# Converting the weights of a fused attention and two-MoE kernel: low parts on VectorE, the first MoE's pieces twice as wide

## The chip, the cores and the metric

The kernel runs on one core of one Trainium2 chip. The metric is the device time of one execution in microseconds (us); lower is better. A core has TensorE (PE, which multiplies matrices; its weight loads are listed apart as PEld), VectorE (DVE), ScalarE (ACT), GpSimd (POOL) and SyncE (SP, which here only issues DMAs). Each engine takes its instructions in the order in which they stand in its queue.

## What is computed

Decay attention, then two feed-forward blocks (the "MoE" of the names), each on the output of the one before:

```python
# attention: batch 4, 8 heads, 576 positions, head size 64
scores = scale * q @ k.T + (cum[:, None] - cum[None, :])   # cum: running sum of log f, causal
x = softmax(scores) @ v                                    # -> 2304 tokens x 512
# first MoE: w_in 512 x 2048, w_out 2048 x 512
h = x @ w_in
x = np.maximum(0.01 * h, h) @ w_out
# second MoE: w_a, w_b 512 x 1536, w_out 1536 x 512
out = ((x @ w_a) * (x @ w_b)) @ w_out
```

The weights arrive as 64-bit floats, eight bytes for each number.

## The kernel before

**Pairs for each product.** PE multiplies in a reduced fp32 format (fp32r). So each operand is kept as two numbers, a high part `hi` and a low part `lo` with hi + lo equal to the value, and each product is three matmuls (hi·hi, hi·lo, lo·hi).

**Converting a weight.** `load_weight` (L105) makes the pair for a block of 128 x 512 numbers, in pieces of `W` columns. For each piece SP fetches the raw doubles into a tile `raw` (L114 or L116), of which there are `RB` buffers. `from_double` (L90) then builds the fp32 number in a tile `c`: ACT takes the absolute value of the upper word (L94), DVE clips it (L95), shifts it (L96), ors bits of the lower word in (L97, which reads `raw` and `c`), and ors the sign in (L100, the same two inputs, and the last reader of `raw`). `split` (L85) writes `hi` on ACT (L87) and `lo = c - hi` (L88), on POOL unless it is told another engine. A `c` tile is free again when its `lo` is written.

**The first MoE's weights** (`load_a`, L523) come in 16 blocks `wi` of w_in and 16 blocks `wo` of w_out, 32 in all, in pieces of 256 columns: 64 pieces, with five buffers of `raw` and three of `c`. They are loaded in the first 186 us, beside the attention of the first tokens and the first matmuls of the MoE. POOL also builds the attention's masks there (L305, L306, L329, L333).

**The second MoE's weights** (`load_b`, L578) are 36 blocks (`wa`, `wb`, `wc`, twelve of each) in one piece of 512 columns each, with three buffers of `raw` and two of `c`. They are loaded from 568 us to about 720 us, beside the last two token chunks (7 and 8) of the first MoE. All blocks but the first few take over the memory of first-MoE blocks, so that their `hi` and `lo` have to wait until PE has used those for the last time.

**The first MoE's matmuls.** For a chunk of 256 tokens and a block fi, `l1` makes h in 12 matmuls (L537); ACT makes `gh` and `hs` from it (L544, L545), and DVE the low part `gl` (L546). `l2` (L559), 12 matmuls as well, runs two or three blocks later. One h and one y together are called a step below. The second MoE's matmuls are L608 and L631.

**Order.** The code is written in an order of its own, and a scheduler then sets the order of the instructions on each engine before the run; nothing is reordered while it runs.

Of the kernel before, what the change touches and what calls it, by code (L numbers as in the profile page):

```python
# [10 lines left out]
I32 = mybir.dt.int32  # L11
# [6 lines left out]
P = 128  # L18
# [8 lines left out]
def kernel(  # L27
# [13 lines left out]
    nc = tc.nc  # L41
    B, H, S, D = q.shape
    NT, DM = out.shape
    w_in, w_out, w_a, w_b, w_o2 = (w.bitcast(I32) for w in (w_in, w_out, w_a, w_b, w_o2))
    F1 = w_in.shape[1] // 2
    F2 = w_a.shape[1] // 2
    NF1, NF2, ND = F1 // P, F2 // P, DM // P
# [10 lines left out]
    wpool = ctx.enter_context(tc.tile_pool(name="wpool", bufs=1))  # L58
# [23 lines left out]
    def f32(ap):  # L82
        return ap.bitcast(F32)

    def split(hi, lo, src, lo_engine=None):  # L85

        nc.scalar.copy(hi, src)  # L87
        (lo_engine or nc.gpsimd).tensor_tensor(out=lo, in0=src, in1=f32(hi), op=ALU.subtract)  # L88

    def from_double(raw, c):  # L90


        top, low, t = raw[:, :, 1], raw[:, :, 0], c.bitcast(F32)
        nc.scalar.activation(t, top.bitcast(F32), AF.Abs)  # L94
        nc.vector.tensor_scalar(t, t, TOP_MIN, TOP_MAX, op0=ALU.max, op1=ALU.min)  # L95
        nc.vector.tensor_scalar(c, c, 5, 2, op0=ALU.logical_shift_left, op1=ALU.logical_shift_right)  # L96
        nc.vector.scalar_tensor_tensor(  # L97
            out=c, in0=low, scalar=29, in1=c, op0=ALU.logical_shift_right, op1=ALU.bitwise_or
        )
        nc.vector.scalar_tensor_tensor(  # L100
            out=c, in0=top, scalar=-0x40000000, in1=c, op0=ALU.bitwise_and, op1=ALU.bitwise_or
        )
        return t

    def load_weight(pool, stg_pool, src, name, W, RB, **kw):  # L105

        hi = pool.tile([P, 512], F32R, tag="w", name=f"{name}_hi", **kw)
        lo = pool.tile([P, 512], F32R, tag="w", name=f"{name}_lo", **kw)
        for z in range(0, 512, W):
            raw = stg_pool.tile([P, W, 2], I32, tag="raw", bufs=RB, name=f"raw_{name}_{z}")  # L110
            view = raw.rearrange("p n t -> p (n t)")
            if len(src.shape) == 3:
                view = view.rearrange("p (a b) -> p a b", b=2 * P)
                nc.sync.dma_start(view, src[:, z // P : (z + W) // P, :])  # L114
            else:
                nc.sync.dma_start(view, src[:, 2 * z : 2 * (z + W)])  # L116
            c = stg_pool.tile([P, W], I32, tag="t", bufs=3 if stg_pool is stage else 2, name=f"c_{name}_{z}")
            split(hi[:, z : z + W], lo[:, z : z + W], from_double(raw, c))
        return hi, lo

    def cols(w, j):

        return w[:, 2 * j * P : 2 * (j + 1) * P].rearrange("(c p) f -> p c f", p=P)

    def rows(w, j):
        return w[j * P : (j + 1) * P, :]
# [5 lines left out]
    stage = stage_ctx.enter_context(tc.tile_pool(name="stage", bufs=2))  # L132
# [389 lines left out]

    def load_a(fi):  # L523
        wa[fi] = (
            *load_weight(wpool, stage, cols(w_in, fi), f"wi_{fi}", 256, 5, bufs=4 * NF1),
            *load_weight(wpool, stage, rows(w_out, fi), f"wo_{fi}", 256, 5, bufs=4 * NF1),
        )

    def l1(i, fi):
# [48 lines left out]
    def load_b(fi):  # L578
        res = []
        for idx, (src, nm) in enumerate(((cols(w_a, fi), "wa"), (cols(w_b, fi), "wb"), (rows(w_o2, fi), "wc"))):  # L580
            pool, bufs = (pools["wx"], 8) if fi * 3 + idx < 4 else (wpool, 4 * NF1)
            res += load_weight(pool, pools["wx"], src, f"{nm}_{fi}", 512, 3, bufs=bufs)
        wb[fi] = res
# [113 lines left out]
    def load_next():  # L697
        nonlocal loaded
        if loaded < NF1:
            load_a(loaded)  # L700
            loaded += 1
# [91 lines left out]
```

## Time and profile before

| | us |
|---|---|
| median of three runs | 1154.49 |
| lowest and highest | 1154.03 to 1155.28 |
| the profiled execution, its whole time | 1155.12 |
| its span in the profile | 1153.3 |
| PE busy in it | 1112.6 |
| DVE busy | 658.0 |
| ACT busy | 571.8 |
| POOL busy | 286.8 |

The span leaves 1.8 us of the execution's time outside it. PE is recorded as busy for 96% of the span, DVE for 57%; these are means over parts with different limits. DVE is busy for nearly all of two stretches, 66 to 186 us (the first MoE's weights) and 604 to 706 us (the second's), and for a few tenths behind 750 us. A matmul's record is longer than the distance to the next one (0.28 us against 0.12 us for 256 columns), so a PE that is recorded as busy can still be short of work; the count of matmuls in a stretch, and the share of its weight loads, show that.

### The profile page before, as it was taken

Reading aid. Unit: us, or ns where it says so; the run is one execution under the profiler, and the core shown is the slowest. Engines: PE = TensorE matmul, PEld = TensorE weight load, DVE = VectorE, ACT = ScalarE, POOL = GpSimd, SP = SyncE. Lnnn points to the kernel's source line nnn. Section 1 sums busy time; section 2 is a strip of 40 time slices with the busy share of each in tenths; the row PEclk is TensorE's granted clock in tenths of the full one; section 3 lists DMA queues with packets and bytes.
Section 4 is the critical chain, followed back from the end, with each engine's and each line's share of the span. In section 5 each row is a group of like instructions: output and inputs, shape, how many; then the busy total and the mean of one; then the engine's idle time right before and its main releaser. Section 6 shows DMA issues by size and latency. Waiting matters only on the chain.

```text
span 1153.3 us, 20360 instructions
## 1 busy us (share of the span) xinstructions
PE 1112.6 (96%) x7021; PEld 981.9 (85%) x7021; DVE 658.0 (57%) x1780; ACT 571.8 (50%) x1511; POOL 286.8 (25%) x486
## 2 busy tenths in 40 slices
PE   6999989999999999999999899999999999999998
PEld 3677778999989999999999887888888888888897
DVE  6789998887878787866459978111111211211122
ACT  5557687888877777867445545212111211211121
POOL 5556553333233323322124324101000100100000
PEclk9999999999999999999999999999999999999999
DMA  7556645433353234521234444101000100100010
GB/s 195 162 150 171 149 121 107 91 79 63 66 122 77 55 69 95 104 51 30 88 115 129 149 143 145 40 1 55 19 1 1 64 1 1 39 8 1 1 37 19
DMA packets 188583, 86.82 MB, mean 75 GB/s; under 512 B 144640, under 2 KB 174336, under 8 KB 188480
## 3 DMA queue, kind: packets, MB, share of 16 engines
q1 hardware_dynamic: 183296, 80.80, 27.9%
q10 hardware_dynamic: 5184, 4.72, 1.2%
q8 instruction: 55, 0.90, 0.3%
q14 instruction: 48, 0.39, 0.1%
HBM read 75.96 MB, written 9.51 MB: 74 GB/s over the span
## 4 chain that ended last, share of the span: by engine, by line
PE 69%; DVE 5%; issue 4%; DMA 3%; ACT 2%; POOL 1%; SPq 0%; ACTq 0%; POOLq 0%; DVEq 0%
PE ab L608 25%; PE o L631 13%; PE h L537 11%; PE y L559 11%; PE av L76 3%; PE s L76 3%; PE pp L76 2%; DMA xk<-in_k_dram 1%; DVE gl L546 1%; DMA sy<-y_dram 1%; DMA y_dram<-yo 1%; DVE c_wc L97 0%; ACT p L283 0%; ACT gh L544 0%; DVE c_wb L97 0%
## 5 line engine op out<-in xcount | busy, mean ns | idle before, releaser
L614 DVE TENSOR_TENSOR p<-ab,p 128x512 f32<-128x512 f32 (+1 forms) x60 | 38.3, 639 | 302.6 <-PE ab L608 299.4
L537 PE MATMUL h<-xh,wi_hi 128*128 128x256 f32 x576 | 168.6, 293 | 8.7 <-ACT hs L545 8.6
L559 PE MATMUL y<-gl,wo_hi 128*128 128x256 f32 x576 | 161.6, 287 | 3.4 <-DVE gl L546 3.4
L537 PE MATMUL h<-xl,wi_hi 128*128 128x256 f32 x576 | 164.7, 286 | 0.0
L537 PE MATMUL h<-xh,wi_lo 128*128 128x256 f32 x576 | 164.6, 286 | 0.0
L559 PE MATMUL y<-gh,wo_lo 128*128 128x256 f32 x576 | 160.5, 285 | 0.0
L559 PE MATMUL y<-gh,wo_hi 128*128 128x256 f32 x576 | 154.4, 292 | 3.9 <-ACT gh L544 3.9
L613 ACT COPY p<-ab 128x512 f32<-128x512 f32 (+1 forms) x60 | 32.7, 545 | 186.3 <-PE ab L608 186.3
L537 PEld LDWEIGHTS h<-xh,wi_hi 128*128 128x128 f32 x576 | 111.2, 193 | 15.7 <-ACT hs L545 12.0
L559 PEld LDWEIGHTS y<-gl,wo_hi 128*128 128x128 f32 x576 | 110.5, 192 | 5.0 <-DVE gl L546 4.3
L305 POOL TENSOR_SCALAR p<-cumb,ncum_t 128x384 f32<-128x384 f32 (+1 forms) x112 | 70.4, 630 | 169.5 <-PE pp L76 41.7
L537 PEld LDWEIGHTS h<-xh,wi_lo 128*128 128x128 f32 x576 | 111.3, 193 | 1.2 <-issue 1.2
L537 PEld LDWEIGHTS h<-xl,wi_hi 128*128 128x128 f32 x576 | 111.5, 194 | 0.8 <-issue 0.4
L559 PEld LDWEIGHTS y<-gh,wo_hi 128*128 128x128 f32 x576 | 104.6, 191 | 7.6 <-ACT gh L544 5.7
L559 PEld LDWEIGHTS y<-gh,wo_lo 128*128 128x128 f32 x576 | 110.7, 192 | 0.4
L87 ACT CAST pph<-p 128x512 fp32r<-128x512 f32 (+1 forms) x60 | 34.7, 578 | 130.5 <-DVE p L614 130.4
L283 ACT ACTIVATE p<-p,stat 128x384 f32<-128x384 f32 (+4 forms) x128 | 77.3, 604 | 26.0 <-DVE stat L312 22.3
L608 PE MATMUL ab<-yh,wb_hi 128*128 128x512 f32 (+1 forms) x240 | 88.8, 370 | 0.7 <-ACT yo L568 0.7
L608 PE MATMUL ab<-yh,wb_lo 128*128 128x512 f32 (+1 forms) x240 | 88.9, 370 | 0.0
L608 PE MATMUL ab<-yl,wa_hi 128*128 128x512 f32 (+1 forms) x240 | 88.8, 370 | 0.0
L608 PE MATMUL ab<-yh,wa_hi 128*128 128x512 f32 (+1 forms) x240 | 88.8, 370 | 0.0
L608 PE MATMUL ab<-yl,wb_hi 128*128 128x512 f32 (+1 forms) x240 | 88.7, 370 | 0.0
(164 smaller groups left out, 2766.3 us busy)
## 6 DMA issues: line engine op xcount, KB each, us to landing
cumb<-cum_dram SPq DMA_DIRECT2D x32, 288.0 KB, 3.7
raw_wi<-in_moe_w_in_dram SPq DMA_DIRECT2D x32, 256.0 KB, 3.1
raw_wo<-in_moe_w_out_dram SPq DMA_DIRECT2D x32, 256.0 KB, 3.2
raw_wa<-in_moe_w_a_dram SPq DMA_DIRECT2D x12, 512.0 KB, 3.6
raw_wb<-in_moe_w_b_dram SPq DMA_DIRECT2D x12, 512.0 KB, 3.5
raw_wc<-in_moe_w_out_dram SPq DMA_DIRECT2D x12, 512.0 KB, 3.6
xq<-in_q_dram SPq DMA_DIRECT2D x144, 32.0 KB, 2.0
y_dram<-yo ACTq DMA_DIRECT2D x36, 128.0 KB, 2.7
```

The costliest lines, as they stand in the source:

```text
L76: return method(*args, **kw)
L87: nc.scalar.copy(hi, src)
L283: act_att.activation(pt, pt, AF.Exp, bias=stat[:, 0, s : s + 1], scale=-1.0, accum_out=stat[:, 1, s : s + 1])
L305: pool_att.tensor_scalar(pt, cumb[:, :n], 1.0, ncum_t[:, t, bh : bh + 1], op0=ALU.mult, op1=ALU.add)
L537: nc.tensor.matmul(hps, w[:, c * P : c * P + P], x[:, c, :], start=(n == 0), stop=(n == 3 * ND - 1))
L546: nc.vector.tensor_tensor(out=gl, in0=hs, in1=f32(gh), op=ALU.subtract)
L559: nc.tensor.matmul(o, w[:, d * P : d * P + P], g, start=(fi == 0 and n == 0 and d % 2 == 0), stop=(fi == NF1 - 1 and n == 2 and d % 2 == 1),)
L608: nc.tensor.matmul(o[:, :tn], w[:, c * P : c * P + P], y[:, c, :tn], start=(m == 0), stop=(m == 3 * ND - 1))
L613: nc.scalar.copy(p[:, :tn], ab[0][:, :tn])
L614: nc.vector.tensor_tensor(out=p[:, :tn], in0=ab[1][:, :tn], in1=p[:, :tn], op=ALU.mult)
L631: nc.tensor.matmul(o, g[:, t * P : t * P + P], w, start=(fi == 0 and m == 0), stop=(fi == NF2 - 1 and m == 2))
```

## The change

Three things change in one place. `split` is told `nc.vector` for all weights, so the `lo` of the 32 + 36 blocks is written by DVE and no longer by POOL. The first MoE's weights are converted in one piece of 512 columns, no longer two of 256. The buffers become two of `raw` (before five, each half as large) and two of `c` (before three, each half as large) for the first MoE; the second MoE's stay at three and two.

```diff
-            c = stg_pool.tile([P, W], I32, tag="t", bufs=3 if stg_pool is stage else 2, name=f"c_{name}_{z}")
-            split(hi[:, z : z + W], lo[:, z : z + W], from_double(raw, c))
+            c = stg_pool.tile([P, W], I32, tag="t", bufs=2, name=f"c_{name}_{z}")
+            split(hi[:, z : z + W], lo[:, z : z + W], from_double(raw, c), nc.vector)
...
-            *load_weight(wpool, stage, cols(w_in, fi), f"wi_{fi}", 256, 5, bufs=4 * NF1),
-            *load_weight(wpool, stage, rows(w_out, fi), f"wo_{fi}", 256, 5, bufs=4 * NF1),
+            *load_weight(wpool, stage, cols(w_in, fi), f"wi_{fi}", 512, 2, bufs=4 * NF1),
+            *load_weight(wpool, stage, rows(w_out, fi), f"wo_{fi}", 512, 2, bufs=4 * NF1),
```

DVE's order in the second MoE's weights, before; a name like `c_wc_6_0` is the tile `c` of block 6 of `wc`, `gl_8_8` the low part of chunk 8, block 8, and the last number only tells instances apart:

```order
L95 TENSOR_SCALAR c_wb_6_0_10773<-c_wb_6_0_10773 128x512
L96 TENSOR_SCALAR c_wb_6_0_10773<-c_wb_6_0_10773 128x512
L97 SCALAR_TENSOR_TENSOR c_wb_6_0_10773<-raw_wb_6_0_10771,c_wb_6_0_10773 128x512
L546 TENSOR_TENSOR gl_8_8_10679<-hs_8_8_10677,gh_8_8_10678 128x256
L100 SCALAR_TENSOR_TENSOR c_wb_6_0_10773<-raw_wb_6_0_10771,c_wb_6_0_10773 128x512
L95 TENSOR_SCALAR c_wc_6_0_10785<-c_wc_6_0_10785 128x512
```

The same place on DVE after the change:

```order
L97 SCALAR_TENSOR_TENSOR c_wb_5_0_10293<-raw_wb_5_0_10291,c_wb_5_0_10293 128x512
L546 TENSOR_TENSOR gl_8_7_10261<-hs_8_7_10259,gh_8_7_10260 128x256
L100 SCALAR_TENSOR_TENSOR c_wb_5_0_10293<-raw_wb_5_0_10291,c_wb_5_0_10293 128x512
L95 TENSOR_SCALAR c_wc_5_0_10305<-c_wc_5_0_10305 128x512
L96 TENSOR_SCALAR c_wc_5_0_10305<-c_wc_5_0_10305 128x512
L88 TENSOR_TENSOR wb_5_lo_10290<-c_wb_5_0_10293,wb_5_hi_10289 128x512
L97 SCALAR_TENSOR_TENSOR c_wc_5_0_10305<-raw_wc_5_0_10303,c_wc_5_0_10305 128x512
L546 TENSOR_TENSOR gl_7_8_10328<-hs_7_8_10326,gh_7_8_10327 128x256
```

The `lo` of a block (L88) now stands between L96 and L97 of the next one, one for each `gl`, as POOL did one for each `gl` before.

DVE's order in the first MoE's weights, around the `gl` of chunk 0, block 8, before:

```order
L342 ISA p4_0_1_4_1572,stat_0_1_4_1412<-s4_0_1_5_1_1799,p4_0_1_4_1572,st4_0_1_5_1791 64x288
L342 ISA stat_0_1_4_1412 64x1
L97 SCALAR_TENSOR_TENSOR c_wi_11_0_1325<-raw_wi_11_0_1323,c_wi_11_0_1325 128x256
L100 SCALAR_TENSOR_TENSOR c_wo_10_256_1236<-raw_wo_10_256_1234,c_wo_10_256_1236 128x256
L243 SCALAR_TENSOR_TENSOR qll_1_0_0_2608<-tq_1_0_0_2605,qhh_1_0_0_2607 128x256
L100 SCALAR_TENSOR_TENSOR c_wi_11_0_1325<-raw_wi_11_0_1323,c_wi_11_0_1325 128x256
L95 TENSOR_SCALAR c_wi_11_256_1335<-c_wi_11_256_1335 128x256
...
L96 TENSOR_SCALAR c_wi_11_256_1335<-c_wi_11_256_1335 128x256
L546 TENSOR_TENSOR gl_0_8_1894<-hs_0_8_1892,gh_0_8_1893 128x256
```

And after:

```order
L97 SCALAR_TENSOR_TENSOR c_wi_12_0_1219<-raw_wi_12_0_1217,c_wi_12_0_1219 128x512
L88 TENSOR_TENSOR wo_11_lo_1114<-c_wo_11_0_1117,wo_11_hi_1113 128x512
L100 SCALAR_TENSOR_TENSOR c_wi_12_0_1219<-raw_wi_12_0_1217,c_wi_12_0_1219 128x512
L342 ISA p4_0_1_4_1312,stat_0_1_4_1172<-s4_0_1_5_1_1499,p4_0_1_4_1312,st4_0_1_5_1491 64x288
L342 ISA stat_0_1_4_1172 64x1
...
L95 TENSOR_SCALAR c_wo_12_0_1231<-c_wo_12_0_1231 128x512
...
L88 TENSOR_TENSOR wi_12_lo_1216<-c_wi_12_0_1219,wi_12_hi_1215 128x512
L96 TENSOR_SCALAR c_wo_12_0_1231<-c_wo_12_0_1231 128x512
...
L546 TENSOR_TENSOR gl_0_8_1574<-hs_0_8_1572,gh_0_8_1573 128x256
```

At the same `gl` the conversion now stands about two blocks further on: block 12 of `wi` has its last step behind it, where block 11 was half done. Ahead of the very first `gl` (chunk 0, block 0) 13 blocks have been converted in DVE's order, before 10.

SP's order at the start of the program, before (`raw_wi_0_256` is the second half of block 0 of `wi`, `cumb` the decay rows that the first masks need):

```order
L114 DMA raw_wi_0_0_187<-in_moe_w_in_dram 128x2x256
L114 DMA raw_wi_0_256_197<-in_moe_w_in_dram 128x2x256
L116 DMA raw_wo_0_0_209<-in_moe_w_out_dram 128x512
L148 DMA cum_dram_58<-cum_93 32x576
...
L275 DMA cumb_0_0_0_121<-cum_dram_58 128x256 x2
L275 DMA cumb_0_0_2_158<-cum_dram_58 128x256 x2
L116 DMA raw_wo_0_256_219<-in_moe_w_out_dram 128x512
L373 DMA vn_0_0_0_229<-in_v_dram 128x2x64 x2
```

And after:

```order
L114 DMA raw_wi_0_0_187<-in_moe_w_in_dram 128x4x256
L116 DMA raw_wo_0_0_199<-in_moe_w_out_dram 128x1024
L373 DMA vn_0_0_0_209<-in_v_dram 128x2x64
L148 DMA cum_dram_58<-cum_93 32x576
...
L373 DMA vn_0_0_0_209<-in_v_dram 128x2x64
L373 DMA vn_0_0_2_325<-in_v_dram 128x2x64
L275 DMA cumb_0_0_0_121<-cum_dram_58 128x256 x2
L275 DMA cumb_0_0_2_158<-cum_dram_58 128x256 x2
```

The second half of the first `wo` block, 256 KB, and three transfers of v now go out ahead of the first `cumb`.

## Rows read from the trace of the kernel before

**Rows 1.** Busy time by stretch: length, busy us and instructions, clock, DMA share, GB/s.
```profile
20.00:66.00 46.00, 44.67 (x142) 28.30 (x143) 34.70 (x119) 27.62 (x92) 26.49 (x48) 1.00 0.61 166
66.00:186.00 120.00, 111.23 (x748) 90.79 (x747) 115.16 (x350) 85.85 (x255) 68.17 (x104) 0.99 0.55 140
186.00:250.00 64.00, 62.73 (x511) 61.79 (x512) 52.60 (x175) 51.54 (x147) 21.85 (x48) 1.00 0.47 97
604.00:664.00 60.00, 55.82 (x444) 53.59 (x443) 57.55 (x86) 31.69 (x70) 23.89 (x17) 1.00 0.45 140
664.00:706.00 42.00, 38.08 (x269) 35.55 (x269) 34.63 (x53) 21.72 (x49) 11.83 (x9) 0.96 0.51 151
706.00:750.00 44.00, 44.00 (x191) 35.41 (x190) 15.95 (x25) 14.12 (x26) 11.06 (x8) 1.00 0.22 64
```
**Rows 2.** Timeline of DVE, one step: start us, us, line, operation.
```profile
639.49 0.41 DVE L546 TENSOR_TENSOR gl<-hs,gh 128x256 fp32r<-128x256 f32 x1
639.82 0.68 DVE L100 SCALAR_TENSOR_TENSOR c_wb<-raw_wb,c_wb 128x512 int32<-128x512 int32 x1
640.42 0.41 DVE L95 TENSOR_SCALAR c_wc<-c_wc 128x512 f32<-128x512 f32 x1
640.87 0.43 DVE L96 TENSOR_SCALAR c_wc<-c_wc 128x512 int32<-128x512 int32 x1
641.34 1.73 DVE L97 SCALAR_TENSOR_TENSOR c_wc<-raw_wc,c_wc 128x512 int32<-128x512 int32 x1
642.99 0.41 DVE L546 TENSOR_TENSOR gl<-hs,gh 128x256 fp32r<-128x256 f32 x1
```
**Rows 3.** Timeline of POOL in the same step (idle before, and what ended it).
```profile
641.24 1.28 POOL L88 TENSOR_TENSOR wb_lo<-c_wb,wb_hi 128x512 fp32r<-128x512 f32 x1 [2.23 <-PE y L559]
```
**Rows 4.** Timeline of DVE where POOL does nothing.
```profile
707.45 0.69 DVE L97 SCALAR_TENSOR_TENSOR c_wa<-raw_wa,c_wa 128x512 int32<-128x512 int32 x1
```
**Rows 5.** Chain of waits, 586 to 590 us: start, us, what.
```profile
586.61 1.44 PE h L537 x12
588.05 1.44 PE y L559 x12
```
**Rows 6.** DVE's groups by shape: count, busy us, mean ns, idle before.
```profile
L88 DVE TENSOR_TENSOR ppl<-p,pph 128x512 fp32r<-128x512 f32 x48 | 34.5, 719 | 32.6 <-ACT pph L87 32.6
L97 DVE SCALAR_TENSOR_TENSOR c_wi<-raw_wi,c_wi 128x256 int32<-128x256 int32 x32 | 17.6, 556 | 0.2
L100 DVE SCALAR_TENSOR_TENSOR c_wi<-raw_wi,c_wi 128x256 int32<-128x256 int32 x32 | 16.3, 514 | 0.1
L95 DVE TENSOR_SCALAR c_wi<-c_wi 128x256 f32<-128x256 f32 x32 | 11.5, 363 | 0.6 <-ACT c_wi L94 0.5
L96 DVE TENSOR_SCALAR c_wi<-c_wi 128x256 int32<-128x256 int32 x32 | 11.0, 347 | 0.2
L88 DVE TENSOR_TENSOR vhl<-vs,vhl 128x512 fp32r<-128x512 f32 x12 | 8.6, 717 | 0.5 <-ACT vhl L87 0.4
```
**Rows 7.** The lines of wi's conversion: ns shortest/median/longest, first and last start.
```profile
L95 DVE TENSOR_SCALAR c_wi<-c_wi x32: 271/288/817, 7.0 to 167.2; 128x256 f32<-128x256 f32 x32
...
L96 DVE TENSOR_SCALAR c_wi<-c_wi x32: 266/284/815, 7.6 to 168.9; 128x256 int32<-128x256 int32 x32
...
L97 DVE SCALAR_TENSOR_TENSOR c_wi<-raw_wi,c_wi x32: 389/423/1234, 8.0 to 170.7; 128x256 int32<-128x256 int32 x32
...
L100 DVE SCALAR_TENSOR_TENSOR c_wi<-raw_wi,c_wi x32: 391/419/971, 9.1 to 172.2; 128x256 int32<-128x256 int32 x32
```
**Rows 8.** DMA issues from the page: count, KB each, median us to landing.
```profile
raw_wi<-in_moe_w_in_dram SPq DMA_DIRECT2D x32, 256.0 KB, 3.1
...
raw_wa<-in_moe_w_a_dram SPq DMA_DIRECT2D x12, 512.0 KB, 3.6
```
**Rows 9.** ACT's groups by shape: count, busy us, mean ns, idle before.
```profile
L94 ACT ACTIVATE c_wa<-raw_wa 128x512 f32<-128x512 f32 x12 | 8.2, 682 | 8.8 <-POOL wb_lo L88 7.2 <-DMA raw_wa<-in_moe_w_a_dram 1.3 <-issue 0.3
```
**Rows 10.** Timeline of POOL at the start: its first mask.
```profile
11.39 0.83 POOL L76 TENSOR_SCALAR p<-cumb,ncum_t 128x128 f32<-128x128 f32 x2 [10.08 <-ACT wo_hi L87]
```

## The prediction

> **What bounds the kernel now.** I read the busy times by stretch first, then DVE's timeline inside the full stretches, then DVE's groups by shape, and last the DMA issues.
>
> By stretch [rows 1], PE's weight loads cover 61.8 of 64 us from 186 to 250 us: there PE has all the work it can take. They cover 90.8 of 120 us from 66 to 186 us, and 53.6 of 60 and 35.6 of 42 us from 604 to 706 us. In the first and second of these short stretches DVE is busy for 115.2 of 120 us and 57.6 of 60 us; in the third, which has a pause for loading y, 34.6 of 42. So the kernel is PE's but for two places, and in both DVE, with the conversion of weights in its queue, holds PE back. I call them A (66 to 186 us, first MoE's weights) and B (604 to 706 us, the second's). Behind 706 us DVE has room again (16.0 of 44 us).
>
> Inside B one step of DVE runs from `gl` to `gl`, 639.49 to 642.99 us [rows 2]: 3.50 us, and its neighbours are alike. PE needs 1.44 + 1.44 = 2.88 us for the same step [rows 5]. Of the 3.50 us L97 takes 1.73 us. It starts 0.10 us behind POOL's `lo` of 1.28 us [rows 3], while the same instruction takes 0.69 us where POOL does nothing [rows 4]. L100, with the same inputs and the same size, takes 0.68 us in the same step. So L97 isn't slow by itself: POOL's `lo` costs DVE 1.73 - 0.69 = 1.04 us in each step.
>
> **The change part by part, B first.** Moving `lo` takes the 1.04 us off DVE and puts a subtraction of two 128x512 tiles on it. Its like is `ppl`, 0.72 us [rows 6]; neighbours on DVE overlap by some 0.08 us (L100's 0.68 us record is followed after 0.60 us), so it costs 0.64 us. The step becomes 3.50 - 1.04 + 0.64 = 3.10 us, still above PE's 2.88. There are 17 + 9 = 26 such POOL instructions in B [rows 1]. Three fall into the pause for y, where DVE isn't the limit: 23 x 0.40 = 9.2 us. Bounds: if DVE waits anew (next paragraph), 3 us; if PE's own floor is reached, since after the change two blocks fewer stand ahead of the last `gl`, 23 x 0.62 = 14 us. I take 8 us, near the lower of the worked-out values, since the pauses stay.
>
> The new wait in B: `lo` can be written only when PE has finished with the block whose memory it takes (POOL waited 2.23 us for PE's y [rows 3]). POOL could wait without harm. On DVE the next L97 and `gl` are queued behind that wait, and ACT's `gh` stands behind ACT's `hi`, which waits for the same blocks. PE's y uses a `gl` three steps later, about 9 us, which covers a wait of a microsecond, and a DVE that runs late finds the memory already free.
>
> **A.** Before, a block of 512 columns is two pieces. By the medians [rows 7] four instructions take 0.288 + 0.284 + 0.423 + 0.419 = 1.41 us, by the means [rows 6] 0.363 + 0.347 + 0.556 + 0.514 = 1.78 us; the 0.37 us between them is stretching by POOL, as in B. Two pieces less eight overlaps of 0.08 us: 2.92 us. After, a block costs 0.41 + 0.43 + 0.69 + 0.68 + 0.72 us less five overlaps, 2.53 us, plus what stretching is left. The attention's masks stay on POOL, so between none and all of the 0.37 us for each of two pieces remains; I take a third, 0.25 us, as the `lo`s go and five instructions stand where eight stood: 2.78 us. For 32 blocks that is 4.5 us less; by the bounds 12.5 us less to 11 us more.
>
> Larger is what moved. Ahead of the first `gl` DVE's order now has 13 blocks, before 10. From the first `gl` to the end of A it has 19 x 2.78 = 52.8 us of conversion in place of 22 x 2.92 = 64.2 us: 11 us less on an engine that is 96% busy. Ahead of it it has 13 x 2.78 - 10 x 2.92 = 7 us more, against 11.3 us of idle time from 20 to 66 us alone, in small pieces, while PE is recorded busy for 44.7 of 46 us. By the bounds of a block it is 2 to 16 us less behind the first `gl`, and 4 to 13 us more ahead of it. I take 8 us of gain for A proper (three quarters of 11, as ACT's and PE's own waits bind too) and 1 us of loss ahead of it (bounds 0 and 7).
>
> PE's recorded busy time leaves only 120 - 111.2 = 8.8 us to win in A. The Trainium skill (Perfetto Trace Analysis, Identifying the Most-Contended Engine) holds that figure to be a poor measure, since matmuls overlap, and goes by the share of weight loads. By that share the room is 29 us and all 11 us could come back, which would make the sum 3 us lower; the value that I take fits under both.
>
> The start: SP now sends the whole first `wo` block and three transfers of v ahead of `cumb`, which the first mask on POOL waits for (11.39 us [rows 10]). That is 256 + 3 x 64 = 448 KB more; at the 166 GB/s that were moved in the next stretch [rows 1], 2.7 us, and at the pace of one 256 KB transfer less than that. I take 1 us of loss (bounds 0 and 2.7).
>
> Narrower things: 64 transfers become 32; ACT issues half as many instructions for the first MoE; POOL loses all 68 blocks and has room. The subtraction on DVE could also be stretched by the masks. The row speaks against much of it: `vhl`, with two inputs of the same size and masks running in those stretches, has a mean of 0.717 us [rows 6]. The Trainium skill (SBUF — State Buffer, SBUF: two separate sides) lets a DVE instruction with two SBUF inputs and a POOL instruction that reads SBUF shut each other out for whole instructions; were half of the 32 subtractions in A held for half a microsecond, A would gain 8 us less. The mean of `vhl` shows no such thing.
>
> **The sum:** 8 (B) + 8 (A) - 1 - 1 = 14 us. The profiled execution took 1155.1 us, 0.6 us above the median of the runs; 1155.1 - 14 = 1141 us.
>
> **The rivals.**
> 1. Only one of the two places gives its gain: A's DVE time is won but PE there waits for ACT or for masks instead (ACT is busy 85.9 of 120 us [rows 1]), or B's steps stay at 3.5 us because DVE waits for memory that PE holds. For it: every engine is in order and closely coupled. Against: DVE is the one that is full. Time: 1155 - 8 + 2 = 1149 us.
> 2. Both gain in full and the start loses nothing: 14 + 11 = 25 us, 1130 us. For it: the room by weight loads. Against: the pause for y and the waits between engines stay.
> 3. Slower: with two buffers of `raw` the loop from L100 to L95 two blocks later shows. SP issues only when L100 has freed the buffer, 512 KB land after 3.6 us [rows 8] where 256 KB took 3.1 us, and ACT's L94 takes 0.7 us [rows 9]: 4.3 us at least, while the attention's loads queue behind that issue on SP, and its exponentials behind L94 on ACT. Before, five smaller buffers let the fetch run two blocks ahead. On the mean there is room, 120 / 19 = 6.3 us for a block in A, so only bunched blocks wait. The point from which it decides: an exposed wait of (8 + 8 - 2) / 32 = 0.44 us for each block cancels the gains. At 0.75 us a block: 1141 + 24 = 1165 us.
> 4. The change doesn't free DVE at all, because L97 is slow for some other reason than POOL's `lo`: then each step of B grows by 0.64 us and A by 32 x 0.64: 1155 + 15 + 20 = 1190 us. Rows 4 speak clearly against it.
>
> **How the numbers follow.** The forecast 0.50, rival 1 0.23, rival 2 0.13, rival 3 0.12, rival 4 0.02. About 0.2%, 2.3 us, is what a measurement can tell from no change. The forecast and rival 2 are faster; of rival 1 most is (0.18), the rest is the same, and so is a mild rival 3 (0.02). Faster 0.81, same 0.07, slower 0.12. The range takes in rival 1 and most of rival 2: 1131 to 1153 us.
>
> **What would show it.** In the profile after: POOL has no L88 for weights; L97 and L100 of `wa`, `wb`, `wc` both near 0.69 us in B; `gl` to `gl` near 3.1 us in the middle of B; more matmuls in each microsecond from 66 to 186 us; the first `gl` at most 2 us later than now, and the last L100 of `wi` ahead of the 172.2 us of now [rows 7]. Wrong would be: ACT's L94 waiting for `raw` for more than 10 us in all, DVE's L88 waiting for PE's y, or PE's first matmul of the MoE several microseconds late.

## The result, and the profile after

The changed kernel takes 1137.4 us (median of four runs, 1136.6 to 1138.3); the kernel before took 1154.3 us beside it. The ratio is 0.985, with a 95% interval of 0.983 to 0.987. Measured again on another chip it was 0.983 (0.981 to 0.986). The forecast was 1141 us. Ratios and intervals here are of executions in the chip's fast state; one slow execution each of experiments 2 and 12 is left out.

The busy line of the page of after, and then its busy time by stretch (length, then busy us and instructions of PE, PEld, DVE, ACT, POOL, then clock, DMA share, GB/s):

```profile
PE 1108.6 (98%) x7021; PEld 979.9 (86%) x7021; DVE 634.9 (56%) x1720; ACT 561.9 (49%) x1447; POOL 197.9 (17%) x386
```

```profile
20.00:66.00 46.00, 44.24 (x144) 29.26 (x143) 38.36 (x107) 28.09 (x78) 18.73 (x33) 1.00 0.74 197
66.00:186.00 120.00, 119.64 (x802) 97.66 (x801) 100.39 (x282) 80.80 (x218) 37.77 (x62) 1.00 0.51 132
186.00:250.00 64.00, 60.87 (x481) 58.39 (x481) 52.45 (x172) 51.40 (x141) 21.53 (x44) 1.00 0.46 87
604.00:664.00 60.00, 60.00 (x503) 60.00 (x502) 51.16 (x104) 32.96 (x77) 0.00 (x0) 1.00 0.53 163
664.00:706.00 42.00, 42.00 (x257) 37.51 (x256) 37.83 (x73) 25.73 (x53) 0.00 (x0) 1.00 0.51 151
```

Against [rows 1]: in B the weight loads now cover all of 604 to 664 us (53.6 before), with 503 matmuls in place of 444. In A they cover 97.7 us (90.8 before), and DVE has come down from 115 to 100 of 120 us. From 186 to 250 us it is the other way: 58.4 us, where there were 61.8.

Stretches by the clock on the wall mix the change of pace with the shift of everything behind it. So I also compared the traces at equal work. Each matmul counts as the distance that its shape usually keeps to the next one. The lead is the difference between the times at which two traces have the same work left:

| lead over the profiled execution before, us, at | 66 | 80 | 186 | 250 | 350 | 568 | 706 | end |
|---|---|---|---|---|---|---|---|---|
| after | 2.7 | -3.3 | 7.3 | 3.2 | 2.1 | 1.4 | 17.7 | 17.8 |
| after, a second time (experiment 9) | 1.6 | 0.0 | 11.6 | 7.5 | 5.3 | 4.2 | 20.5 | 20.6 |
| second MoE's part alone, second time (10) | 0.8 | 0.4 | -0.2 | -1.3 | -0.3 | -0.6 | 15.6 | 15.7 |
| first MoE's part alone (2) | 2.1 | 0.5 | 10.8 | 6.3 | 5.4 | 5.2 | 7.6 | 7.6 |
| lo of wo back on POOL (8) | -1.5 | -3.7 | -2.6 | -1.3 | -5.2 | -6.0 | 10.3 | 10.4 |
| lo of the second's weights also on POOL (5) | 2.1 | -3.8 | 7.8 | 3.7 | 1.5 | 1.6 | 13.8 | 11.5 |
| lo of the second's weights twice on DVE (12) | 2.0 | -4.1 | 7.6 | 3.3 | 1.1 | 0.0 | 16.3 | 16.4 |

The distances of the attention's small matmuls are the weak point of this measure: with the median distance of each shape, the values at 66 us come out up to 3 us apart from these, the others within about 1 us.

This table shows what the total hides. B wins 16 us against this one execution of before, and 14 us by the medians of experiments 1 and 10; the forecast was 8. A wins 7 us by 186 us, loses most of them again by 350 us, and in this execution 1.4 us were left. The two errors nearly cancel.

About 2 of B's 16 us belong to that execution of before: its granted clock fell to 1.2 GHz at 674.3 us for 3.4 us. In experiments 2 and 3, where PE and DVE have the order of before there, the clock reads 1.00 from 664 to 706 us.

DVE's timeline inside B after the change, one step from `gl` to `gl` (start us, us, line, operation):

```profile
632.55 0.42 DVE L546 TENSOR_TENSOR gl<-hs,gh 128x256 fp32r<-128x256 f32 x1
632.89 0.69 DVE L100 SCALAR_TENSOR_TENSOR c_wb<-raw_wb,c_wb 128x512 int32<-128x512 int32 x1
633.49 0.42 DVE L95 TENSOR_SCALAR c_wc<-c_wc 128x512 f32<-128x512 f32 x1
633.95 0.43 DVE L96 TENSOR_SCALAR c_wc<-c_wc 128x512 int32<-128x512 int32 x1
634.29 0.68 DVE L88 TENSOR_TENSOR wb_lo<-c_wb,wb_hi 128x512 fp32r<-128x512 f32 x1
634.89 0.68 DVE L97 SCALAR_TENSOR_TENSOR c_wc<-raw_wc,c_wc 128x512 int32<-128x512 int32 x1
635.49 0.42 DVE L546 TENSOR_TENSOR gl<-hs,gh 128x256 fp32r<-128x256 f32 x1
```

Beside [rows 2]: L97 takes 0.68 us and no longer 1.73, L100 as before, `lo` 0.68 us. The step is 2.94 us, before 3.50. The groups by shape say the same of all the second's blocks, and give the first's (count, busy us, mean ns, idle before):

```profile
L97 DVE SCALAR_TENSOR_TENSOR c_wc<-raw_wc,c_wc 128x512 int32<-128x512 int32 x12 | 8.2, 685 | 0.0
L100 DVE SCALAR_TENSOR_TENSOR c_wa<-raw_wa,c_wa 128x512 int32<-128x512 int32 x12 | 8.2, 687 | 0.1
L88 DVE TENSOR_TENSOR wc_lo<-c_wc,wc_hi 128x512 fp32r<-128x512 f32 x12 | 8.2, 687 | 2.1 <-PE y L559 1.6 <-ACT wc_hi L87 0.4
...
L97 DVE SCALAR_TENSOR_TENSOR c_wi<-raw_wi,c_wi 128x512 int32<-128x512 int32 x16 | 11.3, 704 | 0.1
L100 DVE SCALAR_TENSOR_TENSOR c_wi<-raw_wi,c_wi 128x512 int32<-128x512 int32 x16 | 11.3, 704 | 0.1
L88 DVE TENSOR_TENSOR wi_lo<-c_wi,wi_hi 128x512 fp32r<-128x512 f32 x16 | 11.1, 696 | 0.1
L95 DVE TENSOR_SCALAR c_wi<-c_wi 128x512 f32<-128x512 f32 x16 | 7.1, 446 | 10.6 <-ACT c_wi L94 10.6
L96 DVE TENSOR_SCALAR c_wi<-c_wi 128x512 int32<-128x512 int32 x16 | 7.1, 443 | 0.2
```

The new wait of DVE for PE's y is there once, 1.6 us. The idle time ahead of L95, 10.6 us, is new too: there DVE waits for ACT's L94, and ACT for the fetch.

### The profile page after: what moved, and what is told of

Read it like the earlier page. It is cut to its first block, busy times and chain, and to the rows that moved or that the text cites. A ratio compares the mean times of both kernels' runs of the same rounds, so it can differ in the third digit from the quotient of the medians.

```text
span 1136.1 us, 20019 instructions
## 1 busy us (share of the span) xinstructions
PE 1108.6 (98%) x7021; PEld 979.9 (86%) x7021; DVE 634.9 (56%) x1720; ACT 561.9 (49%) x1447; POOL 197.9 (17%) x386
## 4 chain that ended last, share of the span: by engine, by line
PE 74%; DMA 3%; DVE 3%; SPq 1%; ACT 1%; issue 1%; POOL 0%; DVEq 0%; ACTq 0%; POOLq 0%
PE ab L608 26%; PE o L631 13%; PE y L559 13%; PE h L537 13%; PE av L76 3%; PE s L76 3%; PE pp L76 2%; DMA xq<-in_q_dram 1%; DMA y_dram<-yo 1%; DMA xk<-in_k_dram 1%; DMA cumb<-cum_dram 1%; SPq L236 1%; SPq L234 1%; DVE ks L262 0%; DVE p L312 0%
## 5 line engine op out<-in xcount | busy, mean ns | idle before, releaser
L537 PE MATMUL h<-xh,wi_hi 128*128 128x256 f32 x576 | 165.8, 288 | 0.0
L305 POOL TENSOR_SCALAR p<-cumb,ncum_t 128x384 f32<-128x384 f32 (+1 forms) x112 | 75.9, 679 | 214.1 <-PE pp L76 53.6
L88 POOL TENSOR_TENSOR yl<-sy,yh 128x512 fp32r<-128x512 f32 (+1 forms) x16 | 19.2, 1211 | 408.6 <-ACT yh L87 408.5
L608 PE MATMUL ab<-yh,wa_lo 128*128 128x512 f32 (+1 forms) x240 | 88.7, 370 | 0.0
```

The costliest lines, as they stand in the source:

```text
L305: pool_att.tensor_scalar(pt, cumb[:, :n], 1.0, ncum_t[:, t, bh : bh + 1], op0=ALU.mult, op1=ALU.add)
L537: nc.tensor.matmul(hps, w[:, c * P : c * P + P], x[:, c, :], start=(n == 0), stop=(n == 3 * ND - 1))
L608: nc.tensor.matmul(o[:, :tn], w[:, c * P : c * P + P], y[:, c, :tn], start=(m == 0), stop=(m == 3 * ND - 1))
```

## The experiments

The theory that this suggested, called S in the expectations: B alone makes the time; A's lead is given back, since the attention's chunks come no sooner.

**1 and 2. Each part alone.** Only the second's `lo` on DVE, everything else as before:

```diff
-            split(hi[...], lo[...], from_double(raw, c))
+            split(hi[...], lo[...], from_double(raw, c), None if stg_pool is stage else nc.vector)
```

> Only the second MoE's lo moves to DVE; the first MoE's weights stay in pieces of 256 columns with lo on POOL. DVE's order is then word for word that of before up to the second's weights, and from there that of after. Theory S (read from the two traces by equal remaining TensorE work: the lead of after was 1.4 us at 568 us and 17.7 us at 706 us): nearly the whole gain is in the second's weights, so 1154.3 - 16 = 1138 us, within 2 us of after. The prediction's own split (8 us here, the rest in the first's weights): 1146 us. A theory in which only the two together free DVE: above 1150 us.

Measured: 1141.4 us, a ratio of 0.988 (0.986 to 0.990). Only the first's part (from the changed kernel, with `nc.vector if stg_pool is stage else None`):

> Only the first MoE's part: pieces of 512 columns, two buffers each, lo on DVE; the second's lo stays on POOL. Theory S: the lead of some 7 us that after has at 186 us is given back by 450 us, since the attention's chunks become ready no sooner; the end moves by 1 to 3 us: 1152 to 1153 us. The prediction's split: 8 us minus 2: 1148 us. A rival: the lead survives, since here nothing behind it is changed: 1147 us.

Measured: a ratio of 0.998 (0.995 to 1.001). The executions lay far apart, from 1146.5 to 1158.4 us; the profiled one took 1148.1. So the second's part makes 14 us, and the first's part 2 us with an uncertainty of 3. The prediction's split (8 and 6) doesn't fit. S comes nearer, but it had 16 us for the second's part and no more than 2 us between that and the whole change, which by the ratios is 4 us faster.

**3 and 4. What in the first's part works: the width or the move?** The width alone, lo on POOL as before:

```diff
-            *load_weight(wpool, stage, cols(w_in, fi), f"wi_{fi}", 256, 5, bufs=4 * NF1),
+            *load_weight(wpool, stage, cols(w_in, fi), f"wi_{fi}", 512, 2, bufs=4 * NF1),
...
```

> The first MoE's pieces of 512 columns with two buffers each, but every lo on POOL as before: the size alone. Theory S: whatever it does by 186 us is given back, the end within 2 us of 1154 us. The rival that the gain in the first's weights is that of fewer, longer instructions (eight of 256 columns become four of 512, worth 4 overlaps and heads of some 0.07 us per block): 1150 us. The rival that two buffers of raw expose their fetch: POOL's lo frees c late (1.28 us each), so 1157 us or more.

Measured: 1.001 (0.999 to 1.002). The move alone, pieces of 256 columns, five and three buffers:

> The first MoE's pieces stay at 256 columns with five buffers of raw and three of c, but their lo moves to DVE; the second's stays on POOL: the move alone. DVE gets ten instructions for a block, about 2 x (0.288 + 0.284 + 0.423 + 0.419 + 0.42) - 10 x 0.08 = 2.9 us plus what the masks stretch. Theory S: the end within 2 us of 1154 us. If the move and not the size frees DVE: the lead at 186 us is as large as with both (5 to 7 us), and ACT's wait for raw stays near the 4 us of before, since five buffers stay.

Measured: 1169.1 us, a ratio of 1.016 (1.009 to 1.024): slower. Neither the end within 2 us nor the lead at 186 us came. Its busy time by stretch:

```profile
20.00:66.00 46.00, 42.98 (x174) 27.70 (x174) 32.07 (x121) 26.96 (x87) 17.68 (x36) 0.85 0.57 155
66.00:186.00 120.00, 107.44 (x667) 86.06 (x668) 112.91 (x402) 86.60 (x253) 35.20 (x65) 0.93 0.60 154
186.00:250.00 64.00, 59.14 (x421) 55.44 (x421) 53.12 (x172) 47.69 (x131) 18.88 (x38) 0.90 0.38 79
```

At equal work it was 7 us ahead of before at 66 us and 14 to 17 us behind at 186, by the distances taken. DVE has 402 instructions from 66 to 186 us, where the whole change has 282, and is full again. PE is short of work, and the granted clock falls to a mean of 0.93 there and 0.90 behind it: it went down to 1.2 GHz several times between 154 and 206 us. Its last `lo` ends at 200.7 us, that of before at 181.6. So ten instructions of 256 columns for a block cost DVE more than POOL's `lo` did. How much of the loss is the clock's was not separated. The move needs the width, and the width alone brings nothing.

**5. The price of POOL's subtraction.** On the changed kernel, POOL writes the second's `lo` once more:

```diff
+            if stg_pool is not stage:
+                nc.gpsimd.tensor_tensor(out=lo, in0=f32(c), in1=f32(hi), op=ALU.subtract)
```

> After the change, plus one thing: behind DVE's lo of a block of the second MoE, POOL writes the same lo once more from the same inputs, as it did before. DVE's order stays that of after up to the second's weights. If POOL's subtraction costs DVE 1.04 us each time, as the prediction had it: the L97, L100 or lo that it meets take up to 1.7 us, the blocks of 604 to 690 us need some 24 us more on a DVE that is busy for 51 of 60 us, and the end goes to 1148 to 1156 us. If L97 was long because of something else (its inputs, a wait that counts as busy): L97 stays at 0.69 us and the end at 1138 us.

Measured: 0.991 (0.987 to 0.995), 1143.9 us, 6 us behind the changed kernel at equal work. POOL's timeline there, then DVE's (in this kernel L548 makes `gl`, and POOL's new line is L120):

```profile
628.73 1.35 POOL L120 TENSOR_TENSOR wa_lo<-c_wa,wa_hi 128x512 fp32r<-128x512 f32 x1 [1.03 <-DVE wa_lo L88]
633.56 1.61 POOL L120 TENSOR_TENSOR wb_lo<-c_wb,wb_hi 128x512 fp32r<-128x512 f32 x1 [3.49 <-DVE wb_lo L88]
```

```profile
628.96 1.40 DVE L96 TENSOR_SCALAR c_wb<-c_wb 128x512 int32<-128x512 int32 x1
...
633.34 0.69 DVE L97 SCALAR_TENSOR_TENSOR c_wc<-raw_wc,c_wc 128x512 int32<-128x512 int32 x1
633.94 1.51 DVE L548 TENSOR_TENSOR gl<-hs,gh 128x256 fp32r<-128x256 f32 x1
635.38 0.68 DVE L100 SCALAR_TENSOR_TENSOR c_wc<-raw_wc,c_wc 128x512 int32<-128x512 int32 x1
```

L97 starts 0.22 us ahead of POOL's instruction and takes its 0.69 us. `gl` starts 0.38 us behind it and takes 1.51 us in place of 0.42: it ends 0.28 us after POOL has ended, at 635.17. And POOL's own instruction, which started inside L97, takes 1.61 us and not the 1.28 us of [rows 3]. In the first pair L96 starts 0.23 us behind POOL's instruction and takes 1.40 us, in place of 0.43. So it isn't L97 that was slow: the DVE instruction that starts inside POOL's subtraction waits for its end. The Trainium skill (SBUF — State Buffer, SBUF: two separate sides) says this: an exclusive lock that the first comer keeps for the whole instruction, the other blocking fully. The trace agrees, both ways round, and with the 1.04 us that the prediction read from [rows 2 to 4].

In the second MoE's weights of before and of this kernel a held DVE instruction ends at the same distance behind POOL's each time, wherever it started: 0.28 us for `gl`, L95 and L96, and 0.55 us for L97, L100 and a subtraction of 128x512, which take longer.

The cost at the end is smaller than expected, since the scheduler spread the blocks thinner: 12 blocks (counted by L100) for the 18 `gl` from 606 to 659 us, where after has 15 from 604 to 656. The last conversion came at 736 us and not 705, and PE paid part of it behind 664 us.

**6. The slow start of PE.**

> After the change, plus 24 matmuls: the 12 of the first h (chunk 0, block 0) run three times over into the same bank, so that TensorE has a dense stretch at its first MoE work. In after the first such matmuls follow each other at 0.21 us until 75 us, in before only until 66.5 us, later at 0.12 us. Theory H: that slow pace costs after some 5 us of lead by 80 us, and a dense stretch ends it sooner: the pace of 0.12 us from about 68 us, and a lead of 2 to 5 us over after at 80 us. If the lead is then kept: 1133 to 1135 us; if, as theory S has it, leads won here are given back: 1136 to 1138 us. If the matmuls only cost their time: 1140 to 1142 us.

```diff
-        for c in reversed(range(ND)):
+        for c in [c for _ in range(3 if (i, fi) == (0, 0) else 1) for c in reversed(range(ND))]:
```

Measured: 0.987 (0.984 to 0.990), 1140.6 us. The pace of 0.12 us came at 73 us, not at 68: the scheduler put matmuls of the attention between the extra ones, as it does with the others. No better, and inconclusive on theory H. Experiment 9 shows what the slow pace costs; whether a dense stretch ends it sooner stays open.

**7. The loop of the raw buffers,** which carried the prediction's third rival: one buffer in place of two.

```diff
-            *load_weight(wpool, stage, cols(w_in, fi), f"wi_{fi}", 512, 2, bufs=4 * NF1),
+            *load_weight(wpool, stage, cols(w_in, fi), f"wi_{fi}", 512, 1, bufs=4 * NF1),
...
```

> After the change, but one buffer of raw instead of two for the first MoE's pieces: the price of the loop that the prediction's third case rested on. Each block then needs its fetch (4.0 us to landing), ACT's 0.67 us and DVE's five instructions up to L100 one behind the other, some 7 us, so 32 blocks take about 225 us where they now end at 158 us. If two buffers leave the loop hidden because they halve it to 3.5 us a block against the 5 us that a block has on the mean: one buffer is far above the end of now, 1165 us or more, with ACT's L94 waiting 80 us or more for raw. If the first MoE's weights don't set the end at all: within 5 us of 1138 us.

Measured: 1218.9 us, 1.056 (1.052 to 1.060). The last block is done at 266 us. How long ACT's L94 waited for raw in all (us, times), first in the changed kernel, for wi and wo, then with one buffer:

```profile
  ACT c_wi L94: 16.7, 11
...
  ACT c_wo L94: 11.1, 8
```

```profile
  ACT c_wi L94: 26.9, 14
...
  ACT c_wo L94: 34.0, 14
```

That is 61 us of waiting, less than the 80 expected. The mechanism is real, and the kernel is 82 us slower when it decides; part of that is PE's clock, which has a mean of 0.56 from 186 to 280 us there. With two buffers 28 us of waiting on ACT are left, and DVE feels 15 us of them in 186 us (10.6 ahead of wi's L95, as shown, 4.2 ahead of wo's), as idle time that it can spare.

**8. Half of the first's lo back on POOL** (that of wo).

```diff
-            split(hi[...], lo[...], from_double(raw, c), nc.vector)
+            split(hi[...], lo[...], from_double(raw, c), None if name[:2] == "wo" else nc.vector)
```

> After the change, but the lo of the first MoE's wo blocks goes back to POOL, wi's stays on DVE. DVE has 16 x 0.64 = 10 us less of its own in the first's weights, and up to 16 x 1.0 us of stretching back. If POOL's lo costs DVE more than DVE's own (1.04 against 0.64 us): 3 to 6 us less lead at 186 us, and by theory S at most 2 us of it at the end, 1138 to 1140 us. If the balance of the two engines is what counts: 1133 to 1136 us.

Measured: 0.989 (0.987 to 0.992), 1141.9 us. POOL's 16 instructions make wi's conversion slow, though wi's own lo is on DVE:

```profile
L97 DVE SCALAR_TENSOR_TENSOR c_wi<-raw_wi,c_wi 128x512 int32<-128x512 int32 x16 | 15.1, 943 | 0.2
L100 DVE SCALAR_TENSOR_TENSOR c_wi<-raw_wi,c_wi 128x512 int32<-128x512 int32 x16 | 14.2, 888 | 0.1
```

That is 0.94 and 0.89 us, against 0.70 in after. It is 10 us behind after at 186 us and still 7 us behind at 568 us. Here theory S fails: it allowed 2 us of it at the end. A lead in A is given back only in part.

**9, 10 and 11. The whole change and the second's part side by side,** and another queue for the fetches:

> The changed kernel itself, beside the kernel with the second MoE's part alone on the same chip: what the first MoE's part is worth at the end. The traces by equal remaining TensorE work gave it a lead of 8.3 us at 186 us and 3.2 us at 568 us over that kernel. Theory S (given back, little kept): 2 to 4 us faster than the second part alone, 0.982 to 0.986 of before. If nothing is kept: equal, 0.988. If the whole lead counts: 7 us or more, 0.981 or less.

> The second MoE's part alone, once more, for the comparison in one place: 0.988 of before as it was, 2 to 4 us behind the whole change by theory S, level with it if the first part is worth nothing.

Measured: 1135.6 us, 0.983 (0.981 to 0.986), and 1141.1 us, 0.987 (0.986 to 0.989). So the first's part is worth some 5 us by the medians, with intervals that overlap by a hair; at equal work it is 4.8 us at 568 us of 11.8 us at 186. The executions of the changed kernel lay between 1131.4 and 1142.0 us here. Two of its traces show one cause of that. PE's timeline around 70 us, first the execution of the result, then this one:

```profile
72.95 0.41 PE L537 MATMUL h<-xh,wi_lo 128*128 128x256 f32 x1
73.16 0.41 PE L537 MATMUL h<-xh,wi_hi 128*128 128x256 f32 x1
...
75.42 0.28 PE L559 MATMUL y<-gh,wo_hi 128*128 128x256 f32 x1
75.54 0.28 PE L559 MATMUL y<-gl,wo_hi 128*128 128x256 f32 x1
```

```profile
69.93 0.28 PE L537 MATMUL h<-xh,wi_lo 128*128 128x256 f32 x1
70.05 0.28 PE L537 MATMUL h<-xh,wi_hi 128*128 128x256 f32 x1
```

Matmuls of 256 columns follow each other at 0.21 us until 75 us in the one, which is the lower level of the clock, 1.2 GHz, and only until 65 us in the other; behind that they stand at 0.12 us, the upper one. PE had the same instructions in the same order ahead of it. (The profile's column of the granted clock reads 1.00 in both; here the distance of the matmuls tells. The first clock record of each trace is the rise itself, at 74.9 and 65.1 us.) The second execution was 1.1 us behind the first at 66 us, 3.3 us ahead at 80 us and 2.8 us ahead at the end.

The five traces with this order of A fall into the same two kinds. The clock rose at 64.0 and 65.1 us (experiments 2 and 9), and at 74.9, 75.3 and 76.0 us (the result, 5 and 12); the leads at 80 us are 0.5 and 0.0, and -3.3, -3.8 and -4.1 us. In before and in experiments 1, 3 and 10 it rose at 66.7 to 68.0 us.

> After the change, but the fetches of the first MoE's weights are issued by ACT, right behind the hi of the block whose raw buffer they take, no longer by SP. In after SP waits 42 us in all from 0 to 200 us for the L100 that frees raw, with attention's loads queued behind, and ACT's L94 waits 28 us in all for raw. If SP's order is what makes the wait: ACT's L94 waits under 12 us, and the end is 1 to 5 us sooner, 1133 to 1137 us. If the wait is the loop's own length with two buffers: L94 waits 25 us or more as in after, and the end stays at 1137 to 1139 us. The issues cost ACT up to 32 x 0.4 us = 13 us where it is busy for 81 of 120 us; if ACT is the next limit, 1140 us or more.

```diff
+            fetch = nc.scalar if stg_pool is stage else nc.sync
...
-                nc.sync.dma_start(view, src[:, 2 * z : 2 * (z + W)])
+                fetch.dma_start(view, src[:, 2 * z : 2 * (z + W)])
```

Measured (experiment 11): 0.988 (0.984 to 0.992), 1139.7 us. ACT's L94 still waits:

```profile
  ACT c_wi L94: 22.3, 14
...
  ACT c_wo L94: 8.3, 7
```

30.6 us against 27.8 in after: the wait isn't made by SP's order but by the loop itself, as the second of the expectations had it. Nothing is won; whether the issues cost ACT a microsecond or two can't be told, as the executions lay between 1135.6 and 1150.5 us.

**12. Is DVE still the bound in B?** DVE writes each lo of the second's weights twice.

```diff
+            if stg_pool is not stage:
+                nc.vector.tensor_tensor(out=lo, in0=f32(c), in1=f32(hi), op=ALU.subtract)
```

> After the change, but DVE writes the lo of each block of the second MoE twice: 0.60 us more on DVE for each of 36 blocks. It asks whether DVE still sets the pace there. In after DVE is busy for 51.2 of 60 us from 604 to 664 us, with 15 blocks for 18 low parts gl, and TensorE is full. If TensorE is the bound and DVE has that room: 15 x 0.60 = 9 us more fill it, some blocks slip back behind 704 us, and the end moves by 0 to 4 us: 1136 to 1141 us. If each of DVE's subtractions counts in full, as the prediction's sum of 0.40 us a step had it: 26 x 0.60 = 16 us, 1152 us.

Measured: 0.984 (0.979 to 0.988), median 1138.2 us, 1139.2 us in the profiled execution. Busy time by stretch, first with DVE's second subtraction, then with POOL's (experiment 5):

```profile
604.00:664.00 60.00, 60.00 (x502) 60.00 (x502) 55.65 (x112) 30.79 (x72) 0.00 (x0) 1.00 0.42 129
664.00:706.00 42.00, 42.00 (x263) 37.84 (x263) 34.70 (x67) 22.48 (x47) 0.00 (x0) 1.00 0.52 156
706.00:750.00 44.00, 44.00 (x190) 35.43 (x189) 26.17 (x45) 14.70 (x24) 5.19 (x4) 1.00 0.25 72
```

```profile
604.00:664.00 60.00, 60.00 (x502) 60.00 (x501) 59.45 (x93) 29.91 (x68) 23.28 (x15) 1.00 0.40 121
664.00:706.00 42.00, 41.20 (x256) 36.21 (x255) 33.94 (x51) 20.35 (x46) 10.93 (x8) 1.00 0.47 142
706.00:750.00 44.00, 42.72 (x181) 33.52 (x180) 34.26 (x49) 16.85 (x29) 17.35 (x12) 1.00 0.30 91
```

With the second subtraction on DVE, B's gain is 16.3 us as in after: PE is the bound, and DVE has room for 36 x 0.60 us more. The same subtraction on POOL leaves DVE busy for 59.5 of 60 us with fewer instructions, and costs 6 us. What hurts is not the work but the engine that does it.

## Why the prediction was right, and where it was not

- **The cause in B: right.** L97, L100 and lo are all near 0.69 us, POOL has no L88 for weights, and experiment 5 brings the wait back.
- **The step of B: nearly.** 3.10 us forecast, 2.94 measured. The 0.16 us are overlap. `lo` stands between L96 and L97 of the next block, and starts 0.34 us behind L96; L97, which needs L96's result, started 0.47 us behind it in [rows 2].
- **The size of B: wrong,** 8 us forecast, 14 measured by the medians, the upper bound. The term that failed is "23 x 0.40". It let each step pay for a block, but from 604 to 656 us there are 15 blocks for 18 `gl`: 15 x (2.94 - 0.33) + 18 x 0.33 = 45 us of DVE's time in 51 us, so PE's 2.88 us rule in the mean. A slow step could thus win 0.62 us and not 0.40. But there were only 18 of them in before (13 up to 664 us, 5 behind 680 us), not 23. At equal work the lead grows by 7.1 us from 604 to 664 us and by 2.6 us from 680 to 706 us. So the steps together gave 9.7 us, near the 9.2 of the sum, by two errors.
- **What that sum put at nothing.** The rest of B's 16 us in the trace lies outside the full steps. From 568 to 604 us 2.4 us were won, since there too POOL's `lo` held a `gl`, and PE waited for it:

```profile
579.30 1.47 POOL L88 TENSOR_TENSOR wc_lo<-c_wc,wc_hi 128x512 fp32r<-128x512 f32 x1 [3.35 <-ACT wc_hi L87]
579.55 1.51 DVE L546 TENSOR_TENSOR gl<-hs,gh 128x256 fp32r<-128x256 f32 x1
581.11 0.38 PE L559 MATMUL y<-gl,wo_hi 128*128 128x256 f32 x1 [0.79 <-DVE gl L546]
```

  And the pause for y, which was to stay, gave 4.5 us from 664 to 680 us. The tile `sy`, into which y is loaded (L593), takes its buffer from the same two as `c` (both have the tag "t"). In before the second `sy` goes out when POOL's `lo` has freed a buffer, ACT waits for it, and PE runs dry until 674 us and comes back at the lower clock:

```profile
665.72 1.27 POOL L88 TENSOR_TENSOR wc_lo<-c_wc,wc_hi 128x512 fp32r<-128x512 f32 x1 [2.22 <-ACT wc_hi L87]
667.02 6.93 SPq L594 DMA_DIRECT2D sy<-y_dram  x3
672.25 1.27 ACT L87 CAST yh<-sy 128x512 fp32r<-128x512 f32 x2 [4.56 <-DMA sy<-y_dram]
674.00:677.50 3.50, 3.36 (x16) 3.36 (x17) 2.69 (x6) 1.96 (x5) 0.00 (x0) 0.54 0.26 75
```

  After the change the second `sy` still goes out right behind a `lo`, now DVE's, at 659.64 us, but PE has no gap there: it is busy for 60.0 of 60 us up to 664 us and for 42.0 of 42 us behind it, at a clock of 1.00. Up to 1.7 us of the 4.5 are the 3.4 us at half the clock, which need not come in every execution of before. No run tried the pause by itself.
- **The new wait for PE's y: right,** 1.6 us once.
- **DVE's block in A: nearly.** 0.446 + 0.443 + 0.704 + 0.704 + 0.696 - 5 x 0.08 = 2.59 us for wi, 2.78 taken. The masks stretch less than supposed: some 4 us over the 160 instructions of all 32 blocks, 0.13 us a block, where 0.25 was taken.
- **A's gain: right in its place, wrong at the end.** The lead over before grows by 10.6 us from 80 to 186 us in the profiled execution, where 8 were taken and 11 counted on DVE; up to 1.7 us of it are a fall of the clock to 1.2 GHz for 3.4 us, at 172.5 us, in before. But from 186 to 350 us 5 us of it go again (6 in the second execution), in small waits: PE's weight loads cover 58.4 us of 64 there, 61.8 before. The step that failed is that a lead in A was carried to the end unchanged. Which waits take it back is not isolated. That is nearest to rival 1, where only one place counts at the end; but the waits that it named were in A itself, and its 1149 us were too slow because B gave 14 us and not 8.
- **Ahead of A: right for another reason.** 1 us of loss was forecast for the blocks ahead of the first `gl`. PE's first MoE matmul came sooner, 61.6 us (64.5 before), and the first `gl` 0.8 us later; but PE ran at 1.2 GHz up to 75 us (66.7 before), and 3.5 to 6 us of lead, by the distances taken, went between 66 and 80 us in that execution, at most 1.6 in the other.
- **The start: half right.** The first mask comes at 12.27 us, 0.9 us later than in [rows 10], as forecast. PE was not later for it.
- **Rival 3: real but covered.** ACT waited 28 us for raw. "More than 10 us would be wrong" was the wrong mark: it takes the wait of an engine with room for a loss.
- **The sum.** 8 + 8 - 2 = 14 us was forecast; by the medians 14 from B and 3 to 5 from the first's part beside it make the 17 to 19 measured. The forecast held by luck in its terms: one too small and one too large met.

## What to carry to other kernels

Two engines can lock each other out for whole instructions: before moving work to an idle neighbour, look whether the busy engine's instructions that start inside it grow by what is left of it. Then its price is not its own length but what it holds up. See also which other loads wait for the buffers that it frees. Work out an engine's need over a stretch (instructions of each kind, not one full step times the count), and ask for each gain early in a kernel whether anything behind it is waiting for it.

## What was not expected of the hardware

- A DVE instruction that starts inside POOL's subtraction of two 128x512 tiles is held until that ends: `gl` takes 1.51 us and not 0.42, in the rows above, and ends 0.28 us behind it; L97 takes 1.73 us in [rows 2] and not 0.69, and ends 0.55 us behind it. One-input instructions too: L96 took 1.40 us and not 0.43. Those that read scores from PSUM aren't held: in the trace of before eight L312 started inside a POOL L88, and none took over 2 ns more than the median of its shape elsewhere.
- POOL's masks hold DVE in the same way. In after, L100 starts 0.84 us into a mask, takes 0.99 us in place of 0.69 and ends 0.53 us behind it:

```profile
125.16 1.30 POOL L305 TENSOR_SCALAR p<-cumb,ncum_t 128x384 f32<-128x384 f32 x1 [4.42 <-ACT kn L217]
126.00 0.99 DVE L100 SCALAR_TENSOR_TENSOR c_wi<-raw_wi,c_wi 128x512 int32<-128x512 int32 x1
```

  But masks met few of the conversion's instructions (20 of 160 were stretched by more than 0.08 us), so that the mean of L97 is 0.70 us for wi and 0.73 for wo, against 0.69 in B.
- PE ran at 0.21 us for 256 columns until 64 to 76 us, though the profile has it busy for 44 of 46 us from 20 to 66 us. The end of that differs between executions of one kernel, here by 10 us, and 3 us of it stay to the end. It is one cause of the spread of 1131 to 1142 us. Whether it is the only one is open, as is the larger spread of the first's part alone.
